# q, k and v loads on two DMA queues instead of one, and a new order of the first two chunk pairs

## The chip, the cores and the metric

The kernel runs on one core of a Trainium2 chip. The metric is the time of one execution in microseconds of device time, lower is better. The core has a matrix engine (TensorE: PE, its weight loads PEld), a vector engine (VectorE: DVE), a scalar engine (ScalarE: ACT), a general engine (GpSimd: POOL) and an engine for transfers and waits (SyncE: SP), each with an instruction queue of its own that is worked off in order. Transfers between main memory and the core are carried by 16 DMA engines. A transfer that POOL issues goes through the software queue, one that SP issues through the hardware queue.

## The reference

```python
def _attn_ref(q, k, v):                      # each [4, 8, 768, 64], float32
    B, H, S, D = q.shape
    gamma = 1.0 - 2.0 ** (-5.0 - np.arange(H, dtype=np.float32))
    scale = 1.0 / np.sqrt(D)
    state = np.zeros((B, H, D, D), dtype=np.float32)
    y = np.zeros_like(q)
    for t in range(S):
        state = gamma[None, :, None, None] * state + np.einsum('bhd,bhe->bhde', k[:, :, t], v[:, :, t])
        y[:, :, t] = scale * np.einsum('bhd,bhde->bhe', q[:, :, t], state)
    return y

x = attn_out.transpose(0, 2, 1, 3).reshape(3072, 512)
h = x @ w_in                                 # w_in [512, 2048]
out = (h * np.cos(h)) @ w_out                # w_out [2048, 512]
```

## The kernel before

The recurrence is computed by chunks of 128 steps. A sequence has six chunks, and chunks of two batches are worked on together as a pair p, so there are 12 pairs. Two pairs make a group of 512 tokens, and there are six groups. The second half of the program, the two matrix products around h cos(h), runs on a whole group.

A pair passes through these stages. `load_pair` (L99) fetches q, k and v of two batches, six transfers of 256 KB, whose contiguous runs in main memory are 64 float32, 256 bytes. `conv_q`, `conv_k` and `conv_v` (L139 to L153) cast them to bf16 and multiply the decay into q and v. `stage_t` (L155) transposes q and k on PE into two PSUM banks, and evacuates each bank. `stage_a` (L171) multiplies k and q, `stage_m` (L186) puts the causal mask on the product, on DVE. `stage_y` (L194) makes the output of the pair from the masked product and the state, and brings the state forward. `unit_f` (L229) is one of 16 steps of the first product of a group, with sine on ACT and the product with it on DVE; `unit_o` (L241) is a quarter of one of four tiles of the second product, whose result SP stores in 256 KB transfers.

The order is written by hand: every engine executes its instructions as the program issues them. Ahead of the main loop (L256 to L281) stand the loads of pairs 0 to 4, the four parts of w_in and of w_out (`load_w_in`, L107, `load_w_out`, L112; 512 KB each as bf16, cast on the way from 1 MB of float32) and the whole attention part of pairs 0 and 1. The main loop goes through groups g and 16 steps s each; in each step stands one `unit_f` of group g and one `unit_o` of group g-1, and among them the stages of the next two pairs: at s = 0 and 8 the conversions of a pair (q and v on POOL, k on DVE), at s = 1 and 9 its transposes, at s = 2 and 10 `stage_a`, at s = 6 and 14 `stage_y` and the load of the pair three further on. So pair 2 is converted at g = 0, s = 0, pair 3 at g = 0, s = 8, and pair 4 at g = 1, s = 0.

All loads are issued by POOL. The loads have five buffers (`PRE`), the converted tiles three. Transfers of a queue take turns at eight completion semaphores, so that an issue waits until the transfer eight before it has landed. In names of tiles buffers are numbered: `qf_81` to `qf_85` are the five of q, `kf_86` to `kf_90` of k, `vf_91` to `vf_95` of v, and `qs_98`, `ks_101`, `vs_104` the converted tiles of pair 2; pair 3 uses `qs_96`, `ks_99`, `vs_102`, pair 4 `qs_97`, `ks_100`, `vs_103`.

Of the kernel before, what the change touches and what calls it, by code (L numbers as in the profile page):

```python
# [30 lines left out]
def kernel(  # L31
# [9 lines left out]
    nc = tc.nc  # L41
# [21 lines left out]
    def sb(shape, dt, name):  # L63
        return const.tile(shape, dt, name=name)
# [17 lines left out]
    qf = [sb([128, 2, H, D], FP32, f"qf{i}") for i in range(PRE)]  # L82
    kf = [sb([128, 2, H, D], FP32, f"kf{i}") for i in range(PRE)]
    vf = [sb([128, 2, H, D], FP32, f"vf{i}") for i in range(PRE)]
# [4 lines left out]
    qkt = [sb([128, 2, 2, HP, 128], BF16, f"qkt{i}") for i in range(NB)]  # L89
# [8 lines left out]

    def load_pair(p):  # L99
        bp, c = divmod(p, NC)  # L100
        for t, src in ((qf, q), (kf, k), (vf, v)):
            for b in range(2):
                nc.gpsimd.dma_start(
                    out=t[p % PRE][:, b],
                    in_=src[2 * bp + b, :, ds(c * C, C)].rearrange("h t d -> t h d"))

    def load_w_in(r):  # L107
        nc.gpsimd.dma_start(
            out=w_in_sb[:, :, ts(r, 512)],
            in_=moe_w_in[:, ts(r, 512)].rearrange("(i p) f -> p i f", p=128))  # L110

    def load_w_out(r):  # L112
# [5 lines left out]
    nc.gpsimd.iota(pos, pattern=[[C, NC]], base=1, channel_multiplier=1,  # L118
                   allow_small_or_imprecise_dtypes=True)
    load_pair(0)  # L120
    make_identity(nc, ident)
    nc.vector.memset(lnsc, math.log(scale))
# [13 lines left out]
    def bc(g, c):  # L136
        return g[:, c, :].unsqueeze(2).to_broadcast([128, H, D])

    def conv_q(p, eng):  # L139
        for b in range(2):  # L140
            eng.tensor_tensor(out=qs[p % NB][:, b], in0=qf[p % PRE][:, b],  # L141
                              in1=bc(gq, p % NC), op=ALU.mult)

    def conv_v(p, eng):
        for b in range(2):
            eng.tensor_tensor(out=vs[p % NB][:, b], in0=vf[p % PRE][:, b],  # L146
                              in1=bc(gk, p % NC), op=ALU.mult)

    def conv_k(p, on_act):
        if on_act:  # L150
            nc.scalar.copy(out=ks[p % NB], in_=kf[p % PRE])
        else:
            nc.vector.tensor_copy(out=ks[p % NB], in_=kf[p % PRE])  # L153

    def stage_t(p):  # L155
        n = p % NB
        for b in range(2):
            bank = banks.take()
            tr = bank.bitcast(BF16).rearrange("p (w a t) -> p w a t", w=2, a=HP)
            for w, src in enumerate((qs[n], ks[n])):  # L160
                for a in range(HP):
                    nc.tensor.transpose(tr[:, w, a, :], src[:, b, 2 * a : 2 * a + 2, :], ident)  # L162
            nc.scalar.copy(out=qkt[n][:, b], in_=tr)  # L163
            banks.give(bank)

    def qt(n, b, a):
        return qkt[n][:, b, 0, a, :]

    def kt(n, b, a):
        return qkt[n][:, b, 1, a, :]  # L170
    def stage_a(p):  # L171
        n = p % NB
        todo = []
        for b in range(2):
            bk = [banks.take(), banks.take()]
            ap = [t.rearrange("p (a t) -> p a t", a=HP) for t in bk]
            for a in range(HP):
                for j in range(2):
                    po = 64 * j
                    nc.tensor.matmul(ap[j][:, a, :], lhsT=kt(n, b, a)[po : po + 64, :],  # L180
                                     rhs=qt(n, b, a)[po : po + 64, :],
                                     tile_position=(po, 0))
            todo.append((b, bk, ap))
        return todo

    def stage_m(p, item):  # L186
        b, bk, ap = item
        for j in range(2):
            nc.vector.tensor_tensor(
                out=am[p % 2][b][j], in0=ap[j],  # L190
                in1=mask.unsqueeze(1).to_broadcast([128, HP, 128]), op=ALU.mult)
            banks.give(bk[j])

    def stage_y(p):  # L194
        c = p % NC
        n = p % NB
        for b in range(2):
            bank = banks.take()
            yp = bank.rearrange("p (a t) -> p a t", a=HP)
            for a in range(HP):  # L200
                if c > 0:
                    for j in range(2):
                        nc.tensor.matmul(
                            yp[ts(j, 64), a, :], lhsT=stb[p % 2][:, b, a, ts(j, 64)],
                            rhs=qt(n, b, a), start=True, stop=False,
                            skip_group_check=True)
                for j in range(2):
                    nc.tensor.matmul(
                        yp[ts(j, 64), a, :], lhsT=vs[n][:, b, 2 * a + j, :],
                        rhs=am[p % 2][b][j][:, a, :], start=(c == 0), stop=True,  # L210
                        skip_group_check=True)
            nc.scalar.copy(out=xt[(p // 2) % 2][:, :, ts(2 * (p % 2) + b, C)], in_=yp)
            banks.give(bank)
        if c == NC - 1:
            return
        for b in range(2):
            for a in range(HP):
                for j in range(2):
                    h = 2 * a + j
                    nc.tensor.matmul(  # L220
                        st_ps[ts(j, 64), b, a, :], lhsT=ks[n][:, b, h, :],
                        rhs=vs[n][:, b, h, :], start=(c == 0 and b == 0 and a == 0),
                        stop=True, skip_group_check=True)
        for j in range(2):
            nc.vector.tensor_copy(out=stb[(p + 1) % 2][ts(j, 64), :, :, ts(j, 64)],  # L225
                                  in_=st_ps[ts(j, 64)])


    def unit_f(g, f):  # L229
        bank = banks.take()  # L230
        for i in range(KIN):
            nc.tensor.matmul(bank, lhsT=w_in_sb[:, i, ts(f, 128)], rhs=xt[g % 2][:, i, :],  # L232
                             start=(i == 0), stop=(i == KIN - 1))
        cb = cosb[f % 3]
        nc.scalar.activation(out=cb, in_=bank, func=AF.Sin, bias=halfpi)  # L235
        nc.vector.tensor_tensor(out=gt[g % 2][:, f, :], in0=bank, in1=cb, op=ALU.mult)  # L236
        banks.give(bank)
# [3 lines left out]
    def unit_o(g, j, part):  # L241
        if part == 0:
            o_bank[0] = banks.take()
        bank = o_bank[0]
        for f in range(4 * part, 4 * part + 4):
            nc.tensor.matmul(bank, lhsT=gt[g % 2][:, f, ts(j, 128)], rhs=w_out_sb[:, f, :],  # L246
                             start=(f == 0), stop=(f == KOUT - 1))
        if part == 3:
            o = ob[j % 4]
            nc.scalar.copy(out=o, in_=bank)  # L250
            banks.give(bank)
            bp, c = divmod(2 * g + j // 2, NC)
            nc.sync.dma_start(out=out[ds((2 * bp + j % 2) * S + c * C, C), :], in_=o)


    load_pair(1)  # L256
    for r in range(2):
        load_w_in(r)
    conv_q(0, nc.vector)
    conv_k(0, True)  # L260
    conv_v(0, nc.gpsimd)
    stage_t(0)
    for r in range(2, 4):
        load_w_in(r)
    m0 = stage_a(0)
    conv_q(1, nc.vector)
    conv_k(1, True)
    conv_v(1, nc.gpsimd)
    for it in m0:
        stage_m(0, it)  # L270
    stage_t(1)
    stage_y(0)
    m1 = stage_a(1)
    for it in m1:
        stage_m(1, it)
    load_pair(2)
    load_pair(3)
    stage_y(1)
# [4 lines left out]
    def conv(p):  # L283
        conv_q(p, nc.gpsimd)
        conv_k(p, False)
        conv_v(p, nc.gpsimd)

    todo = []
    for g in range(NG + 1):
        for s in range(16):  # L290
            hf, r = divmod(s, 8)
            p = 2 * (g + 1) + hf
            if g < NG:
                unit_f(g, s)
            if g > 0:
                unit_o(g - 1, *divmod(s, 4))
            if p < NP:
                if r == 0:
                    conv(p)
                elif r == 1:  # L300
                    stage_t(p)
                elif r == 2:
                    todo = stage_a(p)
                    stage_m(p, todo[0])
                elif r == 3:
                    stage_m(p, todo[1])
                elif r == 6:
                    stage_y(p)
                    if p + 3 < NP:
                        load_pair(p + 3)  # L310
# [30 lines left out]
```

## Time and profile before

| what | value |
|---|---|
| median of 3 runs | 254.31 us (254.3 to 255.47) |
| the profiled execution | 254.12 us |
| its span | 252.3 us |
| PE busy | 204.9 us (81%) |
| DVE, ACT, POOL busy | 119.1, 120.1, 116.8 us |
| software queue | 9984 packets, 23.07 MB |
| hardware queue | 3456 packets, 6.29 MB |

The profile is of one execution. Its span runs from the first to the last instruction; the execution's own time is 1.8 us longer. Times in the trace count from the start of the span. The page cuts the span in 40 slices of 6.3 us each and gives the busy share of each engine in tenths, where 9 is 90% or more. MB are those that arrive, so a weight counts as bf16.

### The profile page before, as it was taken

Reading aid. Unit: us, or ns where it says so; the run is one execution under the profiler, and the core shown is the slowest. Engines: PE = TensorE matmul, PEld = TensorE weight load, DVE = VectorE, ACT = ScalarE, POOL = GpSimd, SP = SyncE. Lnnn points to the kernel's source line nnn. Section 1 sums busy time; section 2 is a strip of 40 time slices with the busy share of each in tenths; the row PEclk is TensorE's granted clock in tenths of the full one; section 3 lists DMA queues with packets and bytes.
Section 4 is the critical chain, followed back from the end, with each engine's and each line's share of the span. In section 5 each row is a group of like instructions: output and inputs, shape, how many; then the busy total and the mean of one; then the engine's idle time right before and its main releaser. Section 6 shows DMA issues by size and latency. Waiting matters only on the chain.

```text
span 252.3 us, 4113 instructions
## 1 busy us (share of the span) xinstructions
PE 204.9 (81%) x1640; PEld 107.4 (43%) x1664; DVE 119.1 (47%) x191; ACT 120.1 (48%) x174; POOL 116.8 (46%) x132
## 2 busy tenths in 40 slices
PE   0447400099798999999999999999999999999994
PEld 0336200055354455554455545545555454444441
DVE  4166320029685666347555665375556633343100
ACT  2434500047665556464565565645655554445210
POOL 8999476498999999998330423000000000000000
PEclk9999755569999999999999999999999999999999
DMA  4999999999979689779301110111011101111122
GB/s 110 218 212 207 233 218 209 206 235 219 221 158 222 158 194 223 188 168 221 108 0 44 42 44 1 42 47 42 3 42 44 42 0 44 42 42 42 44 83 83
DMA packets 13458, 29.62 MB, mean 117 GB/s; under 512 B 1664, under 2 KB 5760, under 8 KB 13440
## 3 DMA queue, kind: packets, MB, share of 16 engines
q0 software_dynamic: 9984, 23.07, 44.1%
q1 hardware_dynamic: 3456, 6.29, 6.7%
q8 instruction: 13, 0.21, 0.3%
q14 instruction: 5, 0.04, 0.1%
HBM read 27.26 MB, written 6.29 MB: 133 GB/s over the span
## 4 chain that ended last, share of the span: by engine, by line
PE 67%; POOL 15%; DMA 10%; issue 5%; DVE 1%; ACT 0%; POOLq 0%; ACTq 0%
PE bank_66 L246 14%; PE bank_63 L246 6%; PE bank_65 L232 5%; DMA vf_93<-in_v_dram 5%; PE bank_64 L232 5%; DMA w_out_sb<-in_moe_w_out_dram 5%; PE bank_69 L232 4%; PE bank_67 L232 4%; PE bank_68 L232 4%; PE bank_67 L246 4%; PE bank_63 L232 3%; PE bank_68 L246 3%; PE bank_69 L246 3%; POOL vs_103 L146 1%; POOL vs_102 L146 1%
## 5 line engine op out<-in xcount | busy, mean ns | idle before, releaser
L232 PEld LDWEIGHTS <-w_in_sb 128*128 128x128 bf16 x384 | 36.0, 99 | 40.8 <-issue 2.0
L246 PEld LDWEIGHTS <-gt_120 128*128 128x128 bf16 x192 | 18.8, 98 | 22.6
L246 PEld LDWEIGHTS <-gt_121 128*128 128x128 bf16 x192 | 18.8, 98 | 22.6
L246 PE MATMUL bank_66<-w_out_sb,gt_120 128*128 128x512 bf16 x96 | 24.6, 379 | 0.0
L162 PE MATMUL bank_67<-ident,qs_98 128*128 128x128 bf16 x8 | 1.0, 264 | 22.2 <-POOL qs_98 L141 22.2
L235 ACT ACTIVATE cosb_122<-bank_65,halfpi 128x512 bf16<-128x512 f32 x14 | 9.6, 687 | 14.5 <-PE bank_65 L232 14.5
L246 PE MATMUL bank_66<-w_out_sb,gt_121 128*128 128x512 bf16 x64 | 16.4, 379 | 0.0
L246 PE MATMUL bank_63<-w_out_sb,gt_120 128*128 128x512 bf16 x63 | 16.2, 379 | 0.1
L163 ACT COPY qkt_107<-bank_67 128x1024 bf16<-128x1024 bf16 x2 | 2.0, 1012 | 23.2 <-PE bank_67 L162 23.2
L162 PEld LDWEIGHTS <-qs_98 128*128 128x128 bf16 x32 | 2.4, 106 | 23.6 <-POOL qs_98 L141 22.9
L246 PE MATMUL bank_67<-w_out_sb,gt_121 128*128 128x512 bf16 x48 | 11.8, 379 | 0.0
L236 DVE TENSOR_TENSOR gt_120<-bank_69,cosb_124 128x512 bf16<-128x512 f32 x3 | 2.0, 683 | 19.9 <-ACT cosb_124 L235 19.9
L232 PE MATMUL bank_69<-xt_119,w_in_sb 128*128 128x512 bf16 x44 | 11.3, 379 | 0.0
L225 DVE CAST stb_117<-st_ps 64x512 bf16<-64x512 f32 x12 | 8.2, 687 | 5.7 <-PE st_ps L220 5.5
L235 ACT ACTIVATE cosb_124<-bank_64,halfpi 128x512 bf16<-128x512 f32 x9 | 6.2, 687 | 9.7 <-PE bank_64 L232 9.7
L232 PE MATMUL bank_63<-xt_118,w_in_sb 128*128 128x512 bf16 x40 | 10.3, 379 | 0.0
L232 PE MATMUL bank_65<-xt_119,w_in_sb 128*128 128x512 bf16 x34 | 8.8, 379 | 0.3 <-issue 0.3
L232 PE MATMUL bank_67<-xt_119,w_in_sb 128*128 128x512 bf16 x34 | 8.8, 379 | 0.3 <-issue 0.3
L232 PE MATMUL bank_64<-xt_119,w_in_sb 128*128 128x512 bf16 x34 | 8.8, 379 | 0.3 <-issue 0.3
L232 PE MATMUL bank_65<-xt_118,w_in_sb 128*128 128x512 bf16 x28 | 8.2, 405 | 0.9 <-issue 0.7
L246 PE MATMUL bank_68<-w_out_sb,gt_120 128*128 128x512 bf16 x32 | 8.2, 379 | 0.0
L246 PE MATMUL bank_69<-w_out_sb,gt_121 128*128 128x512 bf16 x32 | 8.2, 379 | 0.0
(324 smaller groups left out, 517.8 us busy)
## 6 DMA issues: line engine op xcount, KB each, us to landing
w_in_sb<-in_moe_w_in_dram POOLq DMA_DIRECT2D x4, 512.0 KB, 9.8
w_out_sb<-in_moe_w_out_dram POOLq DMA_DIRECT2D x4, 512.0 KB, 12.1
qf_81<-in_q_dram POOLq DMA_DIRECT2D x6, 256.0 KB, 4.3
kf_86<-in_k_dram POOLq DMA_DIRECT2D x6, 256.0 KB, 5.0
vf_91<-in_v_dram POOLq DMA_DIRECT2D x6, 256.0 KB, 5.5
qf_82<-in_q_dram POOLq DMA_DIRECT2D x6, 256.0 KB, 5.1
kf_87<-in_k_dram POOLq DMA_DIRECT2D x6, 256.0 KB, 5.8
vf_92<-in_v_dram POOLq DMA_DIRECT2D x6, 256.0 KB, 6.4
```

The lines of the kernel that those rows point to most:

```text
L146: eng.tensor_tensor(out=vs[p % NB][:, b], in0=vf[p % PRE][:, b], in1=bc(gk, p % NC), op=ALU.mult)
L162: nc.tensor.transpose(tr[:, w, a, :], src[:, b, 2 * a : 2 * a + 2, :], ident)
L163: nc.scalar.copy(out=qkt[n][:, b], in_=tr)
L225: nc.vector.tensor_copy(out=stb[(p + 1) % 2][ts(j, 64), :, :, ts(j, 64)], in_=st_ps[ts(j, 64)])
L232: nc.tensor.matmul(bank, lhsT=w_in_sb[:, i, ts(f, 128)], rhs=xt[g % 2][:, i, :], start=(i == 0), stop=(i == KIN - 1))
L235: nc.scalar.activation(out=cb, in_=bank, func=AF.Sin, bias=halfpi)
L236: nc.vector.tensor_tensor(out=gt[g % 2][:, f, :], in0=bank, in1=cb, op=ALU.mult)
L246: nc.tensor.matmul(bank, lhsT=gt[g % 2][:, f, ts(j, 128)], rhs=w_out_sb[:, f, :], start=(f == 0), stop=(f == KOUT - 1))
```

## The change

Of the six loads of a pair SP now issues three (both of q, and the first batch of v), and POOL three (both of k, and the second batch of v). For pairs 0 and 1, the second of the two banks of transposes is evacuated by DVE instead of ACT. In the part ahead of the loop the masks of pair 0 now stand before the conversions of pair 1, and the four w_in loads stand in other places among the stages of pairs 0 and 1. Weights stay on POOL.

```diff
     def load_pair(p):
         bp, c = divmod(p, NC)
-        for t, src in ((qf, q), (kf, k), (vf, v)):
+        for t, src, engs in ((qf, q, (nc.sync, nc.sync)),
+                             (kf, k, (nc.gpsimd, nc.gpsimd)),
+                             (vf, v, (nc.sync, nc.gpsimd))):
             for b in range(2):
-                nc.gpsimd.dma_start(
+                engs[b].dma_start(
                     out=t[p % PRE][:, b],
...
-    def stage_t(p):
+    def stage_t(p, split):
...
-            nc.scalar.copy(out=qkt[n][:, b], in_=tr)
+            if split and b == 1:
+                nc.vector.tensor_copy(out=qkt[n][:, b], in_=tr)
+            else:
+                nc.scalar.copy(out=qkt[n][:, b], in_=tr)
...
     load_pair(1)
-    for r in range(2):
-        load_w_in(r)
+    load_w_in(0)
     conv_q(0, nc.vector)
     conv_k(0, True)
     conv_v(0, nc.gpsimd)
-    stage_t(0)
-    for r in range(2, 4):
-        load_w_in(r)
+    stage_t(0, True)
+    load_w_in(1)
+    load_w_in(2)
     m0 = stage_a(0)
+    for it in m0:
+        stage_m(0, it)
     conv_q(1, nc.vector)
     conv_k(1, True)
     conv_v(1, nc.gpsimd)
-    for it in m0:
-        stage_m(0, it)
-    stage_t(1)
+    load_w_in(3)
+    stage_t(1, True)
     stage_y(0)
...
                 elif r == 1:
-                    stage_t(p)
+                    stage_t(p, False)
```

How this moves instructions is shown at three places. The first is POOL before, where it issues the last loads ahead of the loop and comes to the conversion of pair 2 (`qs_98`). DMASW0 to DMASW7 are the eight semaphores of the software queue.

```order
L113 DMA w_out_sb<-in_moe_w_out_dram 128x4x512 [waits DMASW6_49]
L113 DMA w_out_sb<-in_moe_w_out_dram 128x4x512 [waits DMASW7_49]
L103 DMA qf_85<-in_q_dram 128x8x64 [waits DMASW0_49]
L103 DMA qf_85<-in_q_dram 128x8x64 [waits DMASW1_49]
L103 DMA kf_90<-in_k_dram 128x8x64 [waits DMASW2_49]
L103 DMA kf_90<-in_k_dram 128x8x64 [waits DMASW3_49]
L103 DMA vf_95<-in_v_dram 128x8x64 [waits DMASW4_49]
L103 DMA vf_95<-in_v_dram 128x8x64 [waits DMASW5_49]
L141 TENSOR_TENSOR qs_98<-qf_83,gq 128x512 x2
L146 TENSOR_TENSOR vs_104<-vf_93,gk 128x512 x2
```

Here 38 transfers stand ahead of `qs_98`, and the last waits for the transfer eight before it, the second part of w_out. The same place of POOL in the changed kernel, in which DMAHW0 to DMAHW7 are the semaphores of the hardware queue:

```order
L115 DMA w_out_sb<-in_moe_w_out_dram 128x4x512 [waits DMASW3_49]
L105 DMA kf_90<-in_k_dram 128x8x64 [waits DMASW4_49]
L105 DMA kf_90<-in_k_dram 128x8x64 [waits DMASW5_49]
L105 DMA vf_95<-in_v_dram 128x8x64 [waits DMASW6_49]
L143 TENSOR_TENSOR qs_98<-qf_83,gq 128x512 [waits DMAHW6_49]
L143 TENSOR_TENSOR qs_98<-qf_83,gq 128x512 [waits DMAHW7_49]
L148 TENSOR_TENSOR vs_104<-vf_93,gk 128x512 [waits DMAHW0_49]
L148 TENSOR_TENSOR vs_104<-vf_93,gk 128x512
L105 DMA kf_86<-in_k_dram 128x8x64 [waits DMASW7_49,Activation_49]
L105 DMA kf_86<-in_k_dram 128x8x64 [waits DMASW0_49]
L105 DMA vf_91<-in_v_dram 128x8x64 [waits DMASW1_49,Pool_49]
```

Now 23 transfers stand ahead of `qs_98`, the last of which waits for the second transfer into `kf_89`, and the conversions themselves wait for the hardware queue. The third place is the start of SP's queue, which before held stores of the result only:

```order
L105 DMA qf_81<-in_q_dram 128x8x64 x2
L105 DMA vf_91<-in_v_dram 128x8x64
L105 DMA qf_82<-in_q_dram 128x8x64 x2
L105 DMA vf_92<-in_v_dram 128x8x64
L105 DMA qf_83<-in_q_dram 128x8x64 x2
L105 DMA vf_93<-in_v_dram 128x8x64 [waits DMAHW0_49]
L105 DMA qf_84<-in_q_dram 128x8x64 [waits DMAHW1_49]
L105 DMA qf_84<-in_q_dram 128x8x64 [waits DMAHW2_49]
```

The 15 loads that left POOL stand here, and wait for nothing but the landing of the load eight before.

## Rows read from the trace of the kernel before

**Rows 1.** The page's busy tenths in 40 slices of 6.3 us

```profile
PE   0447400099798999999999999999999999999994
DMA  4999999999979689779301110111011101111122
```

**Rows 2.** Stages: busy us (instructions) of each engine, clock share, DMA share, GB/s

```profile
30.00:51.00 21.00, 0.00 (x0) 0.00 (x1) 1.29 (x2) 0.00 (x0) 13.55 (x17) 0.53 1.12 212
51.00:78.00 27.00, 23.93 (x236) 13.34 (x241) 19.13 (x30) 16.72 (x24) 26.33 (x28) 0.92 0.97 211
78.00:252.00 174.00, 167.99 (x1257) 85.03 (x1273) 85.35 (x130) 90.85 (x134) 51.17 (x54) 1.00 0.29 78
```

**Rows 3.** Waits of the first 80 us: total us, times, longest

```profile
PE bank_67 L162 <- POOL qs_98 L141: 22.2, 1, 22.2
```

**Rows 4.** Timeline of POOL: start us, us, instruction, [idle before it]

```profile
13.01 1.52 POOL L108 DMA_DIRECT2D w_in_sb<-in_moe_w_in_dram  x2
14.52 2.33 POOL L146 TENSOR_TENSOR vs_102<-vf_91,gk 128x512 bf16<-128x512 f32 x2
...
30.92 0.88 POOL L103 DMA_DIRECT2D kf_89<-in_k_dram  x1 [0.32 <-DMA qf_83<-in_q_dram]
32.14 0.88 POOL L103 DMA_DIRECT2D kf_89<-in_k_dram  x1 [0.34 <-DMA qf_83<-in_q_dram]
...
46.11 0.88 POOL L103 DMA_DIRECT2D vf_95<-in_v_dram  x1 [1.25 <-DMA w_out_sb<-in_moe_w_out_dram]
48.99 0.88 POOL L103 DMA_DIRECT2D vf_95<-in_v_dram  x1 [2.00 <-DMA w_out_sb<-in_moe_w_out_dram]
49.89 2.05 POOL L141 TENSOR_TENSOR qs_98<-qf_83,gq 128x512 bf16<-128x512 f32 x2
```

**Rows 5.** DMA of 0 to 20 us, 40 slices of 0.5 us

```profile
GB/s 0 0 0 0 0 0 131 147 262 156 254 287 246 188 213 246 205 221 229 205 213 238 205 221 229 197 229 229 197 221 221 213 213 229 199 172 209 209 205 205
```

**Rows 6.** Loads into vf_95 before 80 us, from issue to landing

```profile
DMA to landing us min/median/max: 11.9/12.7/13.5
```

**Rows 7.** Timelines of PE, DVE and ACT

```profile
51.00 0.61 PE L162 MATMUL bank_67<-ident,qs_98 128*128 128x128 bf16 x4 [22.23 <-POOL qs_98 L141]
62.86 0.39 PE L162 MATMUL bank_69<-ident,qs_96 128*128 128x128 bf16 x4
64.50 0.40 PE L162 MATMUL bank_69<-ident,ks_99 128*128 128x128 bf16 x4 [1.25 <-DVE ks_99 L153]
77.79 0.40 PE L162 MATMUL bank_67<-ident,ks_100 128*128 128x128 bf16 x4 [1.01 <-DVE ks_100 L153]
...
34.35 0.69 DVE L153 CAST ks_101<-kf_88 128x1024 bf16<-128x1024 f32 x1 [5.05 <-DMA kf_88<-in_k_dram]
75.80 0.69 DVE L236 TENSOR_TENSOR gt_121<-bank_68,cosb_122 128x512 bf16<-128x512 f32 x1 [0.81 <-ACT cosb_122 L235]
76.41 1.33 DVE L153 CAST ks_100<-kf_90 128x1024 bf16<-128x1024 f32 x1
...
11.87 1.02 ACT L163 COPY qkt_105<-bank_64 128x1024 bf16<-128x1024 bf16 x1
28.81 0.69 ACT L235 ACTIVATE cosb_123<-bank_66,halfpi 128x512 bf16<-128x512 f32 x1 [0.23 <-PE bank_66 L232]
```

**Rows 8.** Stores: one alone (124 to 128 us, slices of 0.1 us), one among loads

```profile
GB/s 0 0 0 0 0 0 0 0 0 0 0 0 82 348 348 389 369 369 430 246 41 0 0 0 0 0 0 0 0 0 0 0 0 0 0 0 0 0 0 0
out_dram<-ob_126 SPq DMA_DIRECT2D x1, 256.0 KB, 2.0
...
out_dram<-ob_126 SPq DMA_DIRECT2D x1, 256.0 KB, 3.7
124.45 0.33 SPq L253 DMA_DIRECT2D out_dram<-ob_126  x1
```

**Rows 9.** The page's DMA packets and queues: packets, MB, share of 16 engines

```profile
DMA packets 13458, 29.62 MB, mean 117 GB/s; under 512 B 1664, under 2 KB 5760, under 8 KB 13440
q0 software_dynamic: 9984, 23.07, 44.1%
q1 hardware_dynamic: 3456, 6.29, 6.7%
```

**Rows 10.** DMA of 20 to 30 us, 40 slices of 0.25 us

```profile
GB/s 209 201 209 201 209 217 201 213 209 197 209 193 213 266 188 201 193 205 213 193 213 193 209 205 209 209 209 205 209 217 242 328 438 258 242 254 213 246 262 148
```

## The prediction

> **What bounds the kernel now.** Read the busy slices first [rows 1]. TensorE (PE) is full from about 55 us to the end, but idle in slices 5 to 7, while the DMA engines work without a break from the start to about 75 us. The table by stage puts edges on it: between 30 and 51 us PE does nothing and the load rate is 212 GB/s; from 78 us PE is busy 168.0 of 174 us [rows 2]. So what comes after 78 us is PE's own work and stays; a gain has to come from before. The list of waits names the hole: the transposes of pair 2 wait 22.2 us for POOL's conversion `qs_98` [rows 3]. The timeline of POOL says why it is late [rows 4]. POOL converts nothing between 20 and 49.89 us; it issues loads, and each issue waits for a landing. `qs_98` stands behind all 38 transfers of pairs 0 to 4 and the weights, and the queue's eight semaphores let issue n go only when transfer n-8 has landed. The gaps give prices: q, k and v transfers follow each other at 1.22 us (30.92, 32.14), weights at 2.88 us (46.11, 48.99) [rows 4].
>
> These prices rebuild the trace. Data flows from 3.0 us [rows 5]. The last issue, second `vf_95`, waits for the second w_out transfer, with 24 loads and 6 weights landed: 3.0 + 24 x 1.22 + 6 x 2.88 = 49.6 us; the trace has 48.99. The last load of pair 4 should land at 3.0 + 30 x 1.22 + 8 x 2.88 = 62.6; the trace has at most 48.99 + 13.5 = 62.5 [rows 6].
>
> The end hangs on one mark: the `ks_100` transposes of pair 4 at 77.79 us [rows 7], 174.5 us before the end of the span (252.3). I forecast that mark, keep the 174.5 us and add the 1.8 us by which the profiled execution's time (254.1) exceeds its span. The median of the runs, 254.31, is 0.2 above that execution, which is nothing.
>
> **The change, part by part.**
>
> *POOL's queue gets shorter.* Of the 38 issues ahead of `qs_98` 15 go to SP, 23 stay. The last one now waits for the second `kf_89`, so 11 loads and 4 w_in weights must have landed from the software queue, not 24 and 6: 11 x 1.22 + 4 x 2.88 = 24.9 us. The conversions of pair 2 also need three hardware loads of that pair, behind six others. POOL's own issue time to there, 15 x 0.88 + 8 x 0.76 = 19.3 us and about 4.4 us of conversions [rows 4], lies beside the transfers.
>
> *Price of a load on the hardware queue.* No load runs there now. Lower bound: a store of 256 KB there moves at 348 to 430 GB/s [rows 8], so 0.61 us. Upper bound: that queue took 6.7% of 252.3 us on 16 engines for 3456 packets [rows 9], 78 ns each; stores go 2 KB a packet. If loads go by their 256-byte runs at the same price each, 64 on each engine make 5.0 us. The nearest rows are those of the same 256-byte runs on the other queue: 1.22 us in steady flow, and the 242 to 438 GB/s (316 on average, 0.83 us a load) for about 1 us when loads follow weights [rows 10], which says that the engines themselves can do more than the steady flow shows. I take the middle, 1.0.
>
> *Sum.* 3.0 + 24.9 + 9 x 1.0 = 36.9, plus the issue of `vf_95` 0.88: POOL starts `qs_98` at 37.8 where it was 49.89. PE starts 1.1 us later (49.89 to 51.00): 38.9. From there to the mark took 26.8 us and still does: the two waits in it, 1.25 and 1.01 us for `ks_99` and `ks_100` [rows 7], are for casts that stand on DVE behind the products of PE's own last units, whatever POOL does. Mark at 65.7.
> A second path must be done by then: pair 4. Its last load lands at 3.0 + 15 x 1.22 + 15 x 1.0 + 8 x 2.88 = 59.3, against 62.6; with DVE's cast of `ks_100` (1.33 us) it is ready at 61. Before, it lay ready 14 us early; now 5 us, and it is what would be late next. The gain is 77.8 - 65.7 = 12.1 us: 254.1 - 12.1 = **242.0 us**. At 1.22 a load instead, all is 2 us later: 244.
>
> *POOL between pairs 2 and 4.* Loads of pairs 5 and 6 stand there, 3 issues each, not 6. They wait for the w_out landings; the third of pair 6 waits for the first `kf_90`, in the same sum (13 software loads, 8 weights, 15 hardware loads) at 56.9 us, 9 us ahead of the mark.
>
> *SP.* It issues 36 loads besides 24 stores, 0.33 us each [rows 8]. The first 15 loads fill empty buffers; later ones overwrite buffers read two pairs earlier. A store behind a load, or the reverse, delays by part of an issue or of a store's wait, while loads are called for three pairs ahead. Nothing.
>
> *New waits.* `vs_102` now waits for a hardware load as well; behind it on POOL stand w_in 1 to 3 and all of pair 2. With the two queues alternating, 6 loads have landed at 3.0 + 7.3 = 10.3 us and POOL came there at 14.52 [rows 4]. Nothing, unless the hardware queue is starved (below).
>
> *Split evacuation, masks ahead of pair 1, w_in one by one.* Each second copy of ACT (1.0 us) goes to DVE, where the cast of the same shape took 0.69 [rows 7]; bounds are a gain of 2 x 1.0 and a loss of 2 x 0.7 us. All of it ends when PE first has unit 1 done, 28.81 us [rows 7]; the forecast has PE idle until 38.9. That 10 us of idle time covers both ends: zero. If pair 2 came by 31 us the cover would be gone. w_in 1 is needed only three units behind pair 2's transposes, after 41 us; it is the eighth on the software queue, and 6 x 1.22 + 2 x 2.88 with all 15 hardware loads end at 31.1.
>
> **Rivals.**
>
> *The queues add up.* The burst of [rows 10] may mean that a queue is held by its own fetches and that a second one uses the rest. If hardware loads cost 0.61: pair 2 at 3.0 + 24.9 + 5.5 + 0.9 + 1.1 = 35.4, mark 62.2, time 238.5. If they cost nothing beside the other queue: 29.9, PE ready near 31, mark 57.8, time 234. Against it: the load rate sits near 212 GB/s for 21 us on end while a full queue waits [rows 2].
>
> *The hardware queue is served first.* All its 15 loads would be through before the second `kf_89`: 3.0 + 24.9 + 15 x 1.22 + 2.0 = 48.2, mark 75.0, time 251.3. Against it speaks that stores, which are on that queue, do not get through at once beside loads [rows 8].
>
> *The hardware queue is starved.* Software loads go in 4 KB packets: of 13440 under 8 KB 7680 are not under 2 KB, 128 for each of 24 stores and so 64 for each of 72 loads [rows 9]. If hardware loads go in 256-byte ones, and the engines alternate by packet, they move only when the software queue has run dry. A store beside loads took 3.7 us against 2.0 alone [rows 8], which speaks for it. Pair 3 then lands only after the software's 41.3 us and twelve hardware loads: 3.0 + 41.3 + 14.6 = 58.9, its transposes at 60.3, and the mark 14.9 us behind (62.86 to 77.79 [rows 7]): 75.2, time 251.5.
> The Trainium skill, "DMA: Bandwidth & Descriptors", section "Queues, rings and completion order", says that a DMA engine changes between queues only after a whole packet; by that the time would be the 251.5 of this rival, and the 3.7 us of the store agrees without proving it.
>
> *Slower: a hardware load costs more than 2.2 us.* Its place is pair 4, whose last load lands at 3.0 + 15 x 1.22 + 8 x 2.88 + 15 h = 44.3 + 15 h, and whose transposes follow at once. At h = 2.2 this is the present mark, 77.8. At 2.8 it is 86.3 and the time 262.6; at 5.0 it would be 295. For it speaks the packet count of stores, one per contiguous run; against it, that the 19 ns per 256-byte run seen now (1.22 us over 64) already holds a cost beyond bytes.
> The Trainium skill, "DMA: Bandwidth & Descriptors", section "Issuing engines are not separate DMA queues", says that issuing from several engines only saves sequencer time. By that the load rate stays at 215 GB/s and pair 4 lands at 62.6, still ahead of the mark: 244, the sum's other value; no run here shows it yet.
>
> *The change does nothing*: h of about 2.1, or an arbitration that holds pair 2 until 50 us.
>
> **How the numbers follow.** The forecast (237 to 247) has 0.43, adding up 0.17, served first 0.12, starved 0.12, no change 0.04, slower 0.12. Faster by over 0.5% (about what a measurement of this kernel can tell) is 0.84, the same 0.04, slower 0.12. The range runs from 231, the full overlap with the two waits of PE gone too (234 - 2.3), to 254, which leaves out the slow case, no change and little else.
>
> **What would show it.** Right: `qs_98` starts near 38 us, PE's hole is about 10 us, pair 4's transposes come near 65, the load stages stay between 215 and 250 GB/s, and the stretch after is again 174.5 us. Adding up shows as load stages over 250 GB/s. Starvation shows as `qf_81` landing after 10 us with `kf_87` before it, and as a new PE wait at pair 3. Slower shows as waits of PE or POOL for `qf` and `vf` landings of pairs 3 and 4. I am wrong altogether if the tail after pair 4 is no longer full of PE work.

## The result, and the profile after

The changed kernel takes 246.63 us (median of 4 runs, 244.32 to 248.21) against 254.37 for the kernel before: a ratio of 0.9656, interval 0.9583 to 0.9729. In a second set of runs it took 246.63 again (ratio 0.9689, 0.9654 to 0.9725). The forecast was 242.0 with a range from 231 to 254. Times are medians of all runs; the profiled executions of the changed kernel (248.2 us) and of e3 (253.3), e6 (240.5) and e8 (280.1) were longer than most runs of these kernels, so their profiles are read for the order of events, sizes of the changed kernel stand beside those of another execution of 244.6 us (e7), and the ratios leave out runs over 1.5% longer than the fastest.

The page after, the slices that answer to [rows 1], and its DMA packets and queues, which answer to [rows 9]:

```profile
PE   0235630697989999999999999999999999999993
DMA  7999999999979967839124153011101110111112
...
DMA packets 48019, 29.63 MB, mean 120 GB/s; under 512 B 38528, under 2 KB 42624, under 8 KB 48000
q1 hardware_dynamic: 40896, 15.73, 28.5%
q0 software_dynamic: 7104, 13.63, 27.1%
```

PE's hole is now about two slices wide, where it was three and a half, and DMA is as full as before. The hardware queue, 3456 packets before, now has 40896: the 37440 new ones are 1024 for each of 36 loads and 16 small ones each. A load there goes in packets of one 256-byte run, as the bound of the prediction had it; on the software queue it goes in 64 packets of 4 KB.

The table by stage, which answers to [rows 2] (busy us, clock share, DMA share, GB/s):

```profile
30.00:51.00 21.00, 8.68 (x49) 4.10 (x48) 3.87 (x7) 4.80 (x7) 15.31 (x18) 0.67 1.15 204
51.00:78.00 27.00, 24.90 (x247) 13.23 (x246) 21.15 (x35) 18.20 (x27) 17.50 (x18) 1.00 1.04 207
78.00:246.00 168.00, 164.62 (x1226) 81.84 (x1224) 82.14 (x124) 86.65 (x129) 36.75 (x38) 1.00 0.31 82
```

Between 30 and 51 us PE works 8.68 us where it worked none; the load rate is 204 GB/s, no higher than the 212 before. The waits of the first 80 us, and the timelines of POOL and PE (rows 3, 4 and 7 before):

```profile
PE bank_67 L164 <- POOL qs_98 L143: 12.3, 1, 12.3
POOL vs_103 L148 <- DMA vf_92<-in_v_dram: 11.6, 1, 11.6
```

```profile
9.17 1.04 POOL L148 TENSOR_TENSOR vs_102<-vf_91,gk 128x512 bf16<-128x512 f32 x1 [0.63 <-DMA vf_91<-in_v_dram]
11.57 1.04 POOL L148 TENSOR_TENSOR vs_102<-vf_91,gk 128x512 bf16<-128x512 f32 x1 [1.36 <-DMA vf_91<-in_v_dram]
12.56 1.56 POOL L110 DMA_DIRECT2D w_in_sb<-in_moe_w_in_dram  x2
25.75 2.04 POOL L148 TENSOR_TENSOR vs_103<-vf_92,gk 128x512 bf16<-128x512 f32 x2 [11.63 <-DMA vf_92<-in_v_dram]
27.74 0.81 POOL L110 DMA_DIRECT2D w_in_sb<-in_moe_w_in_dram  x1
...
43.29 0.88 POOL L105 DMA_DIRECT2D vf_95<-in_v_dram  x1 [0.29 <-DMA kf_89<-in_k_dram]
44.19 2.05 POOL L143 TENSOR_TENSOR qs_98<-qf_83,gq 128x512 bf16<-128x512 f32 x2
```

```profile
45.30 0.61 PE L164 MATMUL bank_67<-ident,qs_98 128*128 128x128 bf16 x4 [12.32 <-POOL qs_98 L143]
71.73 0.40 PE L164 MATMUL bank_67<-ident,ks_100 128*128 128x128 bf16 x4 [0.70 <-DVE ks_100 L155]
```

PE's wait for `qs_98` fell from 22.2 to 12.3 us, but it ends only 5.7 us earlier (45.30 after 51.00): it also begins later, at 33.0 us where it began at 28.8, because PE got the data of pair 1 later. The mark moved from 77.79 to 71.73 us, and 246.5 - 71.73 = 174.8 us follow it, as 174.5 did before: all of the gain stands in front of the mark, and nothing was given back behind it. But `qs_98` starts at 44.19 us, not at the forecast 37.8. New is POOL's wait of 11.6 us ahead of `vs_103` for the first half of `vf_92`, a hardware load; everything behind it on POOL, from the last w_in to `qs_98`, came later by it.

Why that load was late is in the DMA view of four stretches of this kernel (packets, MB, share of 16 engines): 16 to 23 us, with weights on the software queue; 25 to 26 us, in which the software queue has just run empty; 26 to 29 us, in which it is empty; 37 to 40 us, with q, k and v on both.

```profile
q0 software_dynamic: 1098, 1.09, 91.6%
q1 hardware_dynamic: 1096, 0.28, 29.8%
...
DMA packets 1134, 0.30 MB, mean 301 GB/s; under 512 B 1133, under 2 KB 1133, under 8 KB 1133
...
DMA packets 2516, 0.63 MB, mean 211 GB/s; under 512 B 2516, under 2 KB 2516, under 8 KB 2516
q1 hardware_dynamic: 2516, 0.63, 113.3%
...
q0 software_dynamic: 183, 0.61, 95.1%
q1 hardware_dynamic: 183, 0.05, 12.7%
```

Where both queues have work, the engines take one packet of each in turn: 1098 to 1096, 183 to 183. A hardware packet has 256 bytes, a weight's 1 KB, a software load's 4 KB. So hardware loads move at 40 GB/s beside weights (0.28 MB in 7 us) and at about 16 GB/s beside software loads (183 x 256 bytes in 3 us), and at 211 GB/s alone, after a first microsecond at 301. In the steady flow alone a hardware load costs 0.262 MB / 211 GB/s = 1.24 us, as much as the 1.22 on the other queue; over all four microseconds from 25 to 29 (234 GB/s) it is 1.12.

### The profile page after: what moved, and what is told of

The parts are those of the page before. It is cut to its first block, busy times and chain, and to the rows that moved or that the text cites. A ratio compares the mean times of both kernels' runs of the same rounds, so it can differ in the third digit from the quotient of the medians.

```text
span 246.5 us, 4176 instructions
## 1 busy us (share of the span) xinstructions
PE 209.3 (85%) x1664; PEld 107.8 (44%) x1664; DVE 120.1 (49%) x193; ACT 118.3 (48%) x172; POOL 84.8 (34%) x96
## 3 DMA queue, kind: packets, MB, share of 16 engines
q1 hardware_dynamic: 40896, 15.73, 28.5%
## 4 chain that ended last, share of the span: by engine, by line
PE 69%; DMA 18%; DVE 3%; SPq 2%; POOL 2%; issue 1%; ACT 1%; ACTq 0%; DVEq 0%
PE bank_66 L251 14%; DMA vf_92<-in_v_dram 8%; DMA kf_90<-in_k_dram 6%; PE bank_63 L251 6%; PE bank_65 L237 5%; PE bank_64 L237 5%; PE bank_67 L237 5%; PE bank_69 L237 5%; PE bank_68 L237 5%; DMA kf_89<-in_k_dram 4%; PE bank_67 L251 4%; PE bank_63 L237 4%; PE bank_69 L251 3%; PE bank_68 L251 3%; SPq L105 2%; PE bank_65 L251 1%
## 5 line engine op out<-in xcount | busy, mean ns | idle before, releaser
L251 PE MATMUL bank_66<-w_out_sb,gt_120 128*128 128x512 bf16 x96 | 24.6, 379 | 0.0
L251 PE MATMUL bank_66<-w_out_sb,gt_121 128*128 128x512 bf16 x64 | 16.4, 379 | 0.0
L251 PE MATMUL bank_63<-w_out_sb,gt_120 128*128 128x512 bf16 x64 | 16.4, 379 | 0.0
L251 PE MATMUL bank_67<-w_out_sb,gt_121 128*128 128x512 bf16 x48 | 11.8, 379 | 0.0
L164 PE MATMUL bank_67<-ident,qs_98 128*128 128x128 bf16 x8 | 1.0, 264 | 12.3 <-POOL qs_98 L143 12.3
L237 PE MATMUL bank_69<-xt_119,w_in_sb 128*128 128x512 bf16 x44 | 11.3, 379 | 0.0
L237 PE MATMUL bank_63<-xt_118,w_in_sb 128*128 128x512 bf16 x40 | 10.3, 379 | 0.0
L237 PE MATMUL bank_65<-xt_118,w_in_sb 128*128 128x512 bf16 x32 | 9.1, 410 | 0.3 <-ACT xt_118 L217 0.3
L237 PE MATMUL bank_64<-xt_119,w_in_sb 128*128 128x512 bf16 x36 | 9.3, 380 | 0.0
L237 PE MATMUL bank_65<-xt_119,w_in_sb 128*128 128x512 bf16 x36 | 9.3, 380 | 0.0
L237 PE MATMUL bank_67<-xt_119,w_in_sb 128*128 128x512 bf16 x36 | 9.3, 380 | 0.0
L168 ACT COPY qkt_107<-bank_67 128x1024 bf16<-128x1024 bf16 x2 | 2.0, 1012 | 13.3 <-PE bank_67 L164 13.3
L237 PE MATMUL bank_64<-xt_118,w_in_sb 128*128 128x512 bf16 x32 | 8.2, 380 | 0.0
L237 PE MATMUL bank_68<-xt_118,w_in_sb 128*128 128x512 bf16 x32 | 8.2, 380 | 0.0
L251 PE MATMUL bank_69<-w_out_sb,gt_121 128*128 128x512 bf16 x32 | 8.2, 379 | 0.0
```

## The experiments

Theory A was: POOL's place at the conversion of pair 2 sets the end, its new wait for a starved hardware load holds it up, and the other edits are hidden. The rivals were B, that the new order carries part of the gain, and C, that transfers fill the DMA engines anyway and a wait removed moves nothing.

**e1: the load queues alone; e2: all the rest alone.**

```diff
--- e1, against the kernel before
-        for t, src in ((qf, q), (kf, k), (vf, v)):
+        for t, src, engs in ((qf, q, (nc.sync, nc.sync)),
+                             (kf, k, (nc.gpsimd, nc.gpsimd)),
+                             (vf, v, (nc.sync, nc.gpsimd))):
             for b in range(2):
-                nc.gpsimd.dma_start(
+                engs[b].dma_start(
--- e2, against the changed kernel
...
-                engs[b].dma_start(
+                nc.gpsimd.dma_start(
```

> Only the queues of the loads change; the order ahead of the loop and the evacuation stay as before. Theory A (what matters is where POOL's queue stands at the conversion of pair 2): the other edits lie beside waits for transfers, so this is the changed kernel within 2 us, 244 to 249 us. Theory B (the new order of the weights and masks carries part of the gain): 250 us or more.

> All loads on POOL as before; only the order ahead of the loop and the split evacuation are new. Theory A: POOL comes to the conversion of pair 2 behind the same 38 transfers, near 50 us, so 254 us within 1. Theory B: 252 us or less.

e1 took 246.28 us (ratio 0.9679, 0.9655 to 0.9703), e2 254.2 us (0.9994, 0.9971 to 1.0016). The queues are the whole gain. The split evacuation, the order of the masks and of the w_in loads are worth nothing that can be measured; theory B falls. e1 has the wait for v of pair 1 as well, 10.5 us.

**e3: v of pair 1 converted by DVE; e4: w_in 1 to 3 behind that conversion on POOL.**

```diff
 e3
-    conv_v(1, nc.gpsimd)
+    conv_v(1, nc.vector)
 e4
-    load_w_in(1)
-    load_w_in(2)
     m0 = stage_a(0)
...
     conv_v(1, nc.gpsimd)
-    load_w_in(3)
+    for r in range(1, 4):
+        load_w_in(r)
```

> The changed kernel, but the conversion of v of pair 1 is done by DVE, so that POOL no longer stands 11.6 us before it for a hardware load. Theory A: POOL issues what follows up to 11 us earlier and reaches the conversion of pair 2 at 36 to 40 us instead of 44; 240 to 243 us. Theory C (the DMA engines were busy in that wait with loads that are needed anyway, so order alone moves nothing): 245 to 248 us. If the hardware loads of pair 3 are now the starved ones, the gain comes back as a wait at pair 3 and the time also stays near 246.

> The changed kernel, but w_in parts 1 to 3 are issued behind the conversion of v of pair 1, so that no weights stand in the software queue while the hardware loads of pair 1 run. Theory A with starvation by packets: the first half of v of pair 1 lands near 14 us instead of 25.7, POOL's wait falls from 11.6 us to under 4, the conversion of pair 2 starts at 36 to 40 us and the time is 240 to 243 us. Theory C: 245 to 248 us.

e3 took 248.33 us (ratio 0.9746, 0.9696 to 0.9796), e4 247.57 (0.9728, 0.9703 to 0.9753): neither gained, and both lie near the upper edge of what theory C had given. Theory A in this form fell. POOL's timeline in e3:

```profile
38.38 1.04 POOL L143 TENSOR_TENSOR qs<-qf,gq 128x512 bf16<-128x512 f32 x1 [0.68 <-DMA qf<-in_q_dram]
45.01 1.04 POOL L143 TENSOR_TENSOR qs<-qf,gq 128x512 bf16<-128x512 f32 x1 [5.60 <-DMA qf<-in_q_dram]
53.97 2.04 POOL L148 TENSOR_TENSOR vs<-vf,gk 128x512 bf16<-128x512 f32 x2 [7.91 <-DMA vf<-in_v_dram]
```

POOL did come to pair 2 before 38 us, but its q and v had not landed: in place of one wait for a hardware load it had waits for the next three. In e4 the wait before `vs_103` was 7.3 us and not under 4: w_in 0 still stood in the software queue, and between 16 and 21 us 0.35 MB of it moved. POOL's queue in e4:

```profile
19.71 2.04 POOL L148 TENSOR_TENSOR vs<-vf,gk 128x512 bf16<-128x512 f32 x2 [7.32 <-DMA vf<-in_v_dram]
21.69 2.30 POOL L110 DMA_DIRECT2D w_in_sb<-in_moe_w_in_dram  x3
...
32.65 0.76 POOL L115 DMA_DIRECT2D w_out_sb<-in_moe_w_out_dram  x1 [2.52 <-DMA w_in_sb<-in_moe_w_in_dram]
...
43.41 2.05 POOL L143 TENSOR_TENSOR qs<-qf,gq 128x512 bf16<-128x512 f32 x2
```

POOL was 4 to 6 us earlier at 19.71 than in the two profiles of the changed kernel (23.66 and 25.75), and at 43.41 between the two (40.99 and 44.19): w_in, w_out and k and v loads of pairs 3 and 4 still stood ahead of `qs_98`, and landings of w_in and k paced it.

**e5 and e6: POOL's queue in the order of need.** New theory D: it is neither the wait nor the queue, but which transfers stand ahead of the conversion that PE waits for. In e5 POOL converts pairs 2 and 3 between the loads, ahead of weights that are needed later. `conv` now means q and v alone; k stays where it was, on DVE. Among the stages of pairs 0 and 1 only w_in 0, pair 2 and w_in 1 are loaded; the rest follows behind them. e6 has the same order with all loads on POOL, as in the kernel before.

```diff
     stage_y(1)
+    load_pair(3)
+    conv(2)
+    for r in range(2, 4):
+        load_w_in(r)
+    for r in range(2):
+        load_w_out(r)
+    conv(3)
+    load_pair(4)
+    for r in range(2, 4):
+        load_w_out(r)
+    conv(4)
...
                 if r == 0:
-                    conv(p)
+                    conv_k(p, False)
+                    if p > 4:
+                        conv(p)
```

> The changed kernel with POOL's queue in the order of need: w_in 1 behind the loads of pair 2, the q and v conversions of pair 2 ahead of w_in 2 and 3, those of pair 3 ahead of the loads of pair 4, and w_out split around them. Theory D (three kernels ended within 2 us of each other because the same transfers, many of them not yet needed, stood ahead of what PE waits for; only their order can move the end): conversion of pair 2 at 29 to 34 us, pair 4's transposes at 57 to 63, 233 to 239 us. Theory C (the sum of all transfers up to pair 4 bounds it in any order): pair 4's transposes not before 68 us, 244 us or more.

> The same order of need, but with all loads on POOL as in the kernel before. If the second queue is what gains, this stays above 246 us. If the place of the conversions in POOL's queue is what gains, it ends within 2 us of the split one, 233 to 241 us: 18 loads of 1.22 us and one or two weights of 2.88 us put the conversion of pair 2 at 28 to 33 us.

e5 took 236.55 us (ratio 0.9317, 0.93 to 0.9334), e6 237.56 (0.9346, 0.933 to 0.9362). Both are faster than the kernel before and the changed one. POOL and PE in e5, then in e6:

```profile
19.88 2.04 POOL L148 TENSOR_TENSOR vs<-vf,gk 128x512 bf16<-128x512 f32 x2 [7.33 <-DMA vf<-in_v_dram]
...
27.96 2.07 POOL L143 TENSOR_TENSOR qs<-qf,gq 128x512 bf16<-128x512 f32 x2
...
60.79 0.40 PE L164 MATMUL bank<-ident,ks 128*128 128x128 bf16 x4 [0.48 <-DVE ks L155]
```

```profile
31.44 2.06 POOL L141 TENSOR_TENSOR qs<-qf,gq 128x512 bf16<-128x512 f32 x2
...
59.30 0.40 PE L162 MATMUL bank<-ident,ks 128*128 128x128 bf16 x4 [0.38 <-DVE ks L153]
...
77.92 0.40 PE L162 MATMUL bank<-ident,qs 128*128 128x128 bf16 x4 [1.94 <-POOL qs L141]
```

The transfers are the same as before and none is faster; pair 2 is converted at 28 and 31 us because less stands ahead of it, and the mark moves to 60.8 and 59.3. The wait for v of pair 1 is still there in e5, 7.3 us. Behind the mark 175.1 us follow in e5 as before, but 179.4 in this execution of e6, in which PE waits for POOL's conversion of pair 5 (77.92). With one queue the same order gives nearly all of it; the intervals of the two just meet. That is theory D, and it takes C's bound with it: the sum of all transfers up to pair 4 does not hold the mark at 68 us.

**e7: the changed kernel once more.**

> The changed kernel once more, for a profile beside the others of this job: 244 to 249 us, POOL's conversion of pair 2 between 38 and 45 us, and the time after the transposes of pair 4 again near 174.5 us.

It took 246.63 us (ratio 0.9689, 0.9654 to 0.9725). Its profiled execution was one of 244.63 us:

```profile
23.66 2.04 POOL L148 TENSOR_TENSOR vs<-vf,gk 128x512 bf16<-128x512 f32 x2 [9.69 <-DMA vf<-in_v_dram]
40.99 2.05 POOL L143 TENSOR_TENSOR qs<-qf,gq 128x512 bf16<-128x512 f32 x2
...
59.55 2.04 POOL L148 TENSOR_TENSOR vs<-vf,gk 128x512 bf16<-128x512 f32 x2 [9.18 <-DMA vf<-in_v_dram]
...
67.89 0.40 PE L164 MATMUL bank<-ident,ks 128*128 128x128 bf16 x4 [0.53 <-DVE ks L155]
```

The wait is there as well, 9.7 us, and 242.9 - 67.89 = 175.0 us follow the mark. This execution is 3.6 us shorter than that of the first profile, `qs_98` is 3.2 us earlier and the mark 3.8: the two differ by how the loads fall in the first 41 us. Here POOL waits a second time, 9.2 us for v of pair 3 (59.55); no wait of PE from there to 80 us is longer than 1.2 us.

**e8 and e9: weight rows cut in half**, the first in the changed kernel, the second in e5.

```diff
-        nc.gpsimd.dma_start(
-            out=w_in_sb[:, :, ts(r, 512)],
+        for c in range(2 * r, 2 * r + 2):
+            nc.gpsimd.dma_start(
+                out=w_in_sb[:, :, ts(c, 256)],
...
```

> The changed kernel with every weight transfer cut into two of half the row (256 columns), so that a weight packet has 512 bytes instead of 1 KB; nothing else moves. If the engines alternate packet by packet, hardware loads get a third of the bytes beside weights and not a fifth, some 65 GB/s instead of 40, v of pair 1 lands near 20 us instead of 23 to 26, and POOL's wait for it falls from 10 to 12 us to 5 to 8. If they share by bytes or by time, that wait stays above 9 us. The end should move little either way, 243 to 248 us, since the order of the transfers stays.

> The kernel in the order of need on two queues, with the same halved weight rows. With packets alternating, the hardware loads of pairs 3 and 4 land earlier, but weights later: PE waits less for v of pairs 3 and 4 and more for w_in. 232 to 238 us; over 238 if the 16 issues more cost POOL more than the share brings.

e8's DMA view of 16 to 21 us and POOL's wait:

```profile
DMA packets 2441, 0.92 MB, mean 183 GB/s; under 512 B 1254, under 2 KB 2441, under 8 KB 2441
q0 software_dynamic: 1219, 0.61, 87.9%
q1 hardware_dynamic: 1222, 0.31, 46.7%
...
20.57 2.04 POOL L150 TENSOR_TENSOR vs<-vf,gk 128x512 bf16<-128x512 f32 x2 [5.15 <-DMA vf<-in_v_dram]
```

With packets of 512 bytes the ratio is again one to one, the hardware loads get 0.31 MB in 5 us, 62 GB/s, and the wait is 5.15 us. Packet by packet is shown. The end was missed: e8 took 257.19 us (1.0104, 1.0063 to 1.0145) and e9 242.02 (0.9516, 0.9479 to 0.9554), both slower than with whole rows. In e8 the last issue ahead of `qs_98` waits for a half of w_out, which now lies eight transfers back:

```profile
47.74 0.88 POOL L105 DMA_DIRECT2D vf<-in_v_dram  x1 [1.25 <-DMA w_out_sb<-in_moe_w_out_dram]
48.64 2.05 POOL L145 TENSOR_TENSOR qs<-qf,gq 128x512 bf16<-128x512 f32 x2
```

Eight semaphores hold half as many bytes in flight when the weights are cut, so POOL is bound to later landings. The load rate is lower too, 183 GB/s from 16 to 21 us where whole rows gave 195 (16 to 23 us); how the loss divides between the two was not tried. In e9 it is another place. PE, and the stretch behind the mark (busy us of PE, PEld, DVE, ACT and POOL, clock share, DMA share, GB/s):

```profile
60.43 0.40 PE L166 MATMUL bank<-ident,ks 128*128 128x128 bf16 x4 [1.96 <-DVE ks L157]
64.77 1.89 PE L253 MATMUL bank<-w_out_sb,gt 128*128 128x512 bf16 x4 [1.69 <-DMA w_out_sb<-in_moe_w_out_dram]
...
60.43:80.00 19.57, 17.36 (x132) 8.17 (x133) 8.55 (x13) 8.84 (x13) 17.19 (x19) 0.83 1.19 223
```

The mark comes no later than in e5 (60.43 against 60.79), but 180.0 us follow it and not 175.1: PE waits for halves of w_out, 2.2 us in all, and its granted clock is 0.83 from the mark to 80 us, against 1.00 in e5.

## Why the prediction was right in sign and too large in size

- *POOL's shorter queue is the gain*: right. e1 has all of it, e2 none. PE's hole shrank and the 174.5 us behind the mark stayed (174.8).
- *Price of a hardware load, taken as 1.0*: measured 1.12 to 1.24 alone. At that price nine loads make 1.1 to 2.2 us of the miss. The upper bound's packets of 256 bytes were right, their price of 78 ns was not: at 211 GB/s on 16 engines a 256-byte packet takes 19 ns.
- *New waits: "Nothing, unless the hardware queue is starved"*: this is the step that failed. It looked only at `vs_102`, which did wait little (0.6 and 1.4 us), and not at `vs_103` of pair 1, which also needs a hardware load; and it let the queues alternate evenly by load. They alternate by packet, and `vs_103` waited 9.7 to 11.6 us. `qs_98` came at 41.0 and 44.2, where 37.8 was forecast, 3.2 to 6.4 us late with the price above included, and the mark at 67.9 and 71.7, 2.2 to 6.0 us behind the forecast 65.7. How much of that this one wait cost is not shown: without it (e3) POOL waited for the next hardware loads.
- *From the conversion to the mark 27.9 us*: right within a microsecond, 27.5 (44.19 to 71.73) and 26.9 (40.99 to 67.89).
- *The starved rival*: its mechanism is the one at work, its place was wrong. It put the loss at pair 3; it came at v of pair 1, because POOL stands there in order. POOL's wait for v of pair 3 is seen as well (9.2 us in e7), but PE lost nothing by it: from the transposes of pair 3 to the mark it took 12.8 us, where it was 13.3 before. `qf_81` was not starved, since SP issues it while the software queue is still empty. The Trainium skill, "DMA: Bandwidth & Descriptors", section "Queues, rings and completion order", says that an engine goes round the queues it has work for by whole packets; the counts of 1098 to 1096 and 1219 to 1222 agree.
- *Adding up* and *served first*: both refuted. The load rate between 30 and 51 us is 204 GB/s (210 in e7), below the 212 before; and the hardware queue gets the smaller share, not the first turn.
- *Slower*: did not occur, the price of 1.24 is well under 2.2.
- *Pair 4's last load at 59.3*: too early. In the first profile `vf_95` on SP was issued at 39.25 and landed 30.7 us later, near 70 us (lines below); POOL's conversion of it started at 70.08, and PE did not wait for it.
- *SP, 0.33 us an issue, "nothing"*: some issues were over 20 times as long (last section), and nothing came of it behind the mark.
- What no part of the prediction saw is that the wait is not the bound. Taking it away or cutting it (e3, e4) gained nothing, while e5 gained with a wait of 7.3 us in place: what stands ahead of `qs_98` on POOL is still transfers that PE needs later. What was left to gain lay in their order: 10 us (e5).

What holds the end of e3's runs of 247 us is not shown.

## What to carry to other kernels

When an in-order engine both issues loads and computes, list what stands ahead of the first computation that the matrix engine waits for, and move that computation in front of every transfer that is needed later; this gained 17 us with one queue, where a second queue gained 8. Before splitting loads over two queues compare their packet sizes, since the engines trade packet for packet and the queue with short runs gets only its share. A wait on one starved load is a symptom as long as the transfers behind it are in the wrong order.

## What was not expected of the hardware

The rate of 256-byte runs in steady flow is nearly the same by either queue alone, though one sends 64 packets a load and the other 1024: 211 GB/s on the hardware queue from 26 to 29 us, and 219 on the software queue of the kernel before, from 30 to 40 us, in which it carries only q, k and v:

```profile
DMA packets 666, 2.19 MB, mean 219 GB/s; under 512 B 131, under 2 KB 131, under 8 KB 666
```

For these loads the packet size costs little, but it decides the share; for weights, smaller packets did cost (e8). And an issue on SP, 0.33 us for a store [rows 8], grew long where its loads were starved. SP's timeline in the changed kernel (start, us, one or two issues), and the landing of the two loads into `vf_95`:

```profile
9.08 12.84 SPq L105 DMA_DIRECT2D qf_83<-in_q_dram  x2
...
25.45 2.35 SPq L105 DMA_DIRECT2D qf_84<-in_q_dram  x2
...
39.25 7.84 SPq L105 DMA_DIRECT2D vf_95<-in_v_dram  x1
...
DMA to landing us min/median/max: 18.8/24.8/30.7
```

So a starved queue holds the engine that issues on it as well: 12.84 us for two loads, though these two wait for no semaphore. That is 6.4 us an issue, about what the queue needs to move a load at the 40 GB/s of that stretch (0.262 MB / 40 GB/s = 6.6 us); with the software queue empty (25 to 28 us) an issue took 1.2 us, again about the price of a load. SP had nothing else to do then; what such an issue would cost an engine that also computes was not tried.
